# Turning two token blocks of a transformer kernel's prologue on VectorE and with SBUF to SBUF DMAs instead of on TensorE

## The chip, the cores and the metric

The kernel runs on one core of one Trainium2 chip. The metric is device time in microseconds of one execution, here the median of several runs. The core's engines have their own instruction queues, each worked off in order: TensorE (PE, with its weight loads shown as PEld), VectorE (DVE), ScalarE (ACT), GpSimd (POOL) and SyncE (SP), which only issues DMAs. They wait for each other through semaphores. Operands lie in SBUF (128 partitions); TensorE writes to PSUM, which has eight banks of 128x512 float32.

## The reference

Two rounds of an attention block followed by a Fourier mixing block, each behind a layer norm and with a residual. S = 2048 tokens, D = 640 columns, H = 32 heads of 20 columns, all float32.

```python
def _A_ref(x, wqkv, wo):
    qkv = (x @ wqkv).reshape(B, S, 3, H, Dh)      # then q, k, v by head
    scores = jnp.einsum("bhqd,bhkd->bhqk", q, k) * (Dh ** -0.5)
    p = _softmax(scores, axis=-1)
    o = jnp.einsum("bhqk,bhkd->bhqd", p, v)
    return o.transpose(0, 2, 1, 3).reshape(B, S, D) @ wo
...
x = A_x
x = x + _A_ref(_layernorm(x, axis=-1), A_wqkv, A_wo)
x = x + _B_ref(_layernorm(x, axis=-1), B_dft_seq_re, B_dft_seq_im, B_dft_hid_re, B_dft_hid_im)
x = x + _A_ref(_layernorm(x, axis=-1), A_wqkv, A_wo)
x = x + _B_ref(_layernorm(x, axis=-1), B_dft_seq_re, B_dft_seq_im, B_dft_hid_re, B_dft_hid_im)
```

## The kernel before

Each of the two layers has a **prologue**, the attention proper, a projection and the Fourier part. The change touches the prologue, function `prologue` of class `Qkv`.

The prologue works on four blocks `tb` = 0 to 3 of 512 tokens; a block is four tiles of 128 tokens, loaded two at a time (`load(k)`, k = 2 tb and 2 tb + 1, into tiles `xa`). A pair is normalised in two steps: VectorE computes mean and variance (`stats`, BN_STATS and BN_AGGR, finished on POOL as `ars`), and ScalarE applies them in place (`norm`, L132). For the matrix products the tokens must lie along the free dimension, so `turn(tb)` transposes the block: for each of the ND = 5 chunks of 128 columns four TensorE transposes of 128x128 into one PSUM bank (`ptr`, L169), then `split` takes the 512 columns out of PSUM into the tile `xt` as a high part (a copy on ScalarE, L90) and a low part (a subtraction on VectorE, L91). Each float32 product is made of three matmuls: high by high, high by low, low by high (`passes`, L103).

With `xt` of a block TensorE makes two products `pqk` of 30 matmuls each in pairs (15 for the first chunk of q, 15 for that of k; the timeline merges them as x30) and four value tiles `pv` of 15 matmuls (`own`, x60). `keep` brings a pqk tile to SBUF (`hl`, L220 on ScalarE, L222 and L223 on VectorE) and POOL stores it to DRAM (`scrq`, `scrk`, L224); ScalarE copies the value tiles to `v` (L265). A small matmul `pn` takes norms.

The order is the order of the code, which is kept on each engine. In round `tb` of the loop TensorE runs: pqk of block tb, then (for tb at least 1) `turn(tb + 1)`, pn, and the value tiles of block tb. In round 0 the value tiles come before the turn. In round tb the loop also calls `stats` and `norm` for the two pairs of block tb + 2. So in round 1 VectorE takes, in this order, the subtraction of the first pqk (L223), statistics, the squares' maximum (L222) and subtraction of the second pqk, statistics, and the five subtractions of the turned block; ScalarE takes the copies of pqk, the five copies of the turned block, four normalisations, and the value tiles. SyncE, after the two loads of x, issues in round 0 eight loads of q from DRAM (`qload`: `stq`, L522 and L523), in round 1 a weight load (L191) and eight loads of k (`kload`: `stk`, L508 and L509), in round 2 another weight load (L191) and a store of zeros (L536).

PSUM tiles of the prologue go round the eight banks in the order in which they are made. A DMA issued by SyncE signals one of eight semaphores in turn, and waits for the DMA before on the same semaphore. The tiles v15 to v11 of the pool `vals` hold raw weights until the value weights are split, and are set up as value tiles by `ones` (memsets on POOL) in round 1.

Of the kernel before, what the change touches and what calls it, by code (L numbers as in the profile page):

```python
# [5 lines left out]
F32 = mybir.dt.float32  # L6
F32R = mybir.dt.float32r
# [8 lines left out]
S, D, H, DH = 2048, 640, 32, 20  # L16
# [3 lines left out]
ND = D // 128  # L20
# [19 lines left out]
def mha_fnet_kernel(ctx, tc, x_in, wqk, wv, wo, seq, hid, nat_seq, nat_hid, out):  # L40
# [44 lines left out]
    def split(hl_h, hl_l, src, vector=False):  # L85

        if vector:
            V.tensor_copy(hl_h, src)  # L88
        else:
            A.activation(hl_h, src, AF.Copy)  # L90
        V.tensor_tensor(hl_l, src, hl_h.bitcast(F32), op=OP.subtract)  # L91
# [39 lines left out]
    def normed(dst, x, rs, i):  # L131
        A.activation(dst, x, AF.Identity, scale=rs[:, 0, i:i + 1], bias=rs[:, 1, i:i + 1])  # L132
# [5 lines left out]
    class Qkv:  # L138
        def __init__(s, L, src):
            s.L, s.src = L, src  # L140
            s.xn, s.xt, s.rs, s.v, s.sq = {}, {}, {}, {}, {}
# [3 lines left out]
            s.made, s.raw, s.silent = set(), {}, False  # L145


        def load(s, k):

            s.xn[k] = (s.first if k % 4 < 2 else s.room)(f"x{k % 4}", [2, D], F32, "xa")  # L150
# [15 lines left out]
        def turn(s, tb, wait=False):  # L166

            def transpose(p, i, dc):
                PE.transpose(p[:, i * 128:(i + 1) * 128],  # L169
                             s.xn[2 * tb + i // 2][:, i % 2, dc * 128:(dc + 1) * 128], ident)  # L170

            ps = [s.bank([128, 512], "ptr") for _ in range(ND if wait else 0)]
            for i in range(4 if wait else 0):
                for dc in range(ND):
                    transpose(ps[dc], i, dc)
            for dc in range(ND):
                if wait:
                    p = ps[dc]
                else:
                    p = s.bank([128, 512], "ptr")  # L180
                    for i in range(4):
                        transpose(p, i, dc)
                x = s.xtp(f"xt{tb}_{dc}", [2, 512], F32R, "xt")
                s.xt[tb, dc] = [x[:, 0], x[:, 1]]
                split(x[:, 0], x[:, 1], p)

        def fetch(s, c, room=None, tag="wraw", wait=False):
            s.raw[c] = (room or s.fill)(tag, [ND, 128], F32, "wraw")
# [83 lines left out]
        def begin(s, first, kq, vals, room, given):  # L272


            s.first, s.room, s.given, s.w = first, room, given, {}
            for k in range(2):
                if given:
                    s.raw[k * ND] = given.wraw[k]
                else:
                    s.load(k)  # L280
            s.wvraw = [vals(f"v{NT - 1 - dc}", [HD], F32, "wvraw") for dc in range(ND)]
            if given:
                s.load_values()

        def take(s, k):

            s.xn[k] = s.first(f"x{k}", [2, D], F32, "xa")
            for i in range(2):
                normed(s.xn[k][:, i], s.given.x[2 * k + i][:, 0], s.given.next[k], i)

# [4 lines left out]
        def prologue(s, vals, xt, fill, att):  # L295
# [39 lines left out]
            def later(tb, k, f):  # L335
                if tb + 2 < NB:
                    f(2 * tb + 4 + k)

            def own(tb, n, between=None):
                t = 4 * tb + n  # L340
                p = s.bank([128, HD], "pv")
                for dc in range(ND):
                    for f in s.value(p, t, dc):
                        f()
                    if between and dc == 1:
                        between()
                s.own(p, t, 0, False)

            for tb in range(NB):

                sq, late, last = {}, tb == 0, tb == NB - 1
                if late:
                    for k in range(2):
                        later(tb, k, s.load)
                for k in (1, 0) if last else (0, 1):
                    p = s.bank([128, 512], "pqk")
                    for dc in range(ND):
                        for f in s.product(p, s.w[k], tb, dc):
# [12 lines left out]
                if tb == 0:  # L371
                    att.setup()
                elif tb == 1:
                    for t in range(NT - ND, NT):
                        ones(t)
                if tb + 1 < NB:
                    s.turn(tb + 1)
                    for k in range(2):
                        later(tb + 1, k, s.load)
                for k in range(1 if last else 0, 2):  # L380
                    later(tb, k, s.norm)
                    s.norms(s.bank, k * ND, tb, sq[k])
                if tb == 0:
                    att.qload(0, 0, None)
                elif tb == 1:
                    s.fetch(ND + 1)
                    for j in range(2):
                        att.kload(0, 0, j)
                elif tb == 2:
                    s.w1 = s.weights(s.fill("w", [2, ND, 128], F32R, "wqk"), ND + 1, True)  # L390
                    s.fetch(1)
                    att.zeros(room)

                def bounds():
                    s.norms(s.bank, 0, tb, sq[0])
                    list(s.bound(0, room))
                    att.qshift(0, 0)
                    for j in range(2):
                        att.kload(0, 1, j)

                if not late:
                    for n in range(4):
                        own(tb, n, bounds if last and n == 0 else None)
            s.made |= {0, ND}


# [1237 lines left out]
```

## Time and profile before

| | us |
|---|---|
| median of 3 runs | 2447.15 (2446.68 to 2448.31) |
| the profiled execution | 2448.28 |
| its span, first to last instruction | 2446.5 |
| end of the last pv matmul of the prologue of layer 0 (76.79 + 8.18) | 84.97 |
| granted TensorE clock, mean | 0.998 of full speed |

The profile is of one execution. Its rows name a line of the kernel, the engine, the operation and the tiles (out<-in). A timeline row gives the start in microseconds from the start of the span, the duration, and what ran; x is the number of instructions merged in it; brackets give how long the engine was idle before and what ended that. SPq rows are DMA issues on SyncE's queue. Matmuls are pipelined, so that the starts tell more than the durations. The prologue of layer 1 lies at about 1220 to 1297 us, with the same order.

### The profile page before, as it was taken

Reading aid. Unit: us, or ns where it says so; the run is one execution under the profiler, and the core shown is the slowest. Engines: PE = TensorE matmul, PEld = TensorE weight load, DVE = VectorE, ACT = ScalarE, POOL = GpSimd, SP = SyncE. Lnnn points to the kernel's source line nnn. Section 1 sums busy time; section 2 is a strip of 40 time slices with the busy share of each in tenths; the row PEclk is TensorE's granted clock in tenths of the full one; section 3 lists DMA queues with packets and bytes.
Section 4 is the critical chain, followed back from the end, with each engine's and each line's share of the span. In section 5 each row is a group of like instructions: output and inputs, shape, how many; then the busy total and the mean of one; then the engine's idle time right before and its main releaser. Section 6 shows DMA issues by size and latency. Waiting matters only on the chain. (4 is left out here: it accounts for less than half of the span.)

```text
span 2446.5 us, 43831 instructions
## 1 busy us (share of the span) xinstructions
PE 2423.7 (99%) x16320; PEld 1167.8 (48%) x16320; DVE 996.3 (41%) x2250; ACT 2114.9 (86%) x2428; POOL 530.7 (22%) x1036
## 2 busy tenths in 40 slices
PE   8999999999999999999999999999999999999998
PEld 7644444443333332339885444454433333333496
DVE  6244442234343333428753444323433332333275
ACT  6699998899999999995457999988999999999862
POOL 2022211112212212115421212211111211222143
PEclk9999999999999999999999999999999999999999
DMA  5324231223232225318552332312221322252265
GB/s 186 101 88 127 83 111 53 77 69 111 73 95 90 87 89 164 98 38 293 196 181 96 112 102 86 117 54 70 78 82 57 93 63 69 57 153 79 77 240 198
DMA packets 128226, 262.63 MB, mean 107 GB/s; under 512 B 29936, under 2 KB 54288, under 8 KB 128004
## 3 DMA queue, kind: packets, MB, share of 16 engines
q1 hardware_dynamic: 89412, 159.89, 20.2%
q0 software_dynamic: 38592, 99.85, 12.8%
q8 instruction: 131, 2.15, 0.4%
q14 instruction: 91, 0.75, 0.1%
HBM read 175.29 MB, written 84.31 MB: 106 GB/s over the span
## 5 line engine op out<-in xcount | busy, mean ns | idle before, releaser
L547 ACT ACTIVATE e<-psc 128x1024 f32<-128x1024 f32 x2048 | 1917.3, 1060 | 108.8 <-PE psc L544 98.2
L555 PE MATMUL acc<-e,v 128*32 128x512 f32 x8192 | 1030.0, 600 | 0.4 <-DVE of L562 0.4
L544 PE MATMUL psc<-stq,stk 62*128 62x512 f32 x4096 | 746.7, 445 | 1.9 <-ACT e L547 0.5
L544 PEld LDWEIGHTS psc<-stq,stk 62*128 62x128 f32 x4096 | 334.2, 184 | 704.8 <-ACT e L547 567.7
L555 PEld LDWEIGHTS acc<-e,v 128*32 128x32 f32 x8192 | 211.0, 108 | 407.2 <-issue 369.7
L103 PE MATMUL pqk<-xt,wqk 128*128 128x512 f32 x1200 | 319.1, 407 | 0.4 <-DVE xt L91 0.4
L576 POOL DMA_DIRECT2D o<-oh x256 | 131.8, 523 | 825.0 <-DVE oh L571 813.1
L88 DVE CAST hl<-pqk 128x512 fp32r<-128x512 f32 x64 | 44.3, 692 | 603.7 <-PE pqk L103 603.7
L103 PEld LDWEIGHTS pqk<-xt,wqk 128*128 128x128 f32 x1200 | 213.2, 188 | 83.5 <-issue 39.5
L103 PE MATMUL pv<-wv,xt 128*128 128x320 f32 x960 | 151.7, 313 | 0.0
L103 PEld LDWEIGHTS pv<-wv,xt 128*128 128x128 f32 x960 | 141.0, 188 | 13.5 <-issue 9.7
L562 DVE STREAM_TRANSPOSE of<-acc 128x512 f32<-128x512 f32 x64 | 45.8, 715 | 225.3 <-PE acc L555 225.3
L576 POOL DMA_DIRECT2D o<-ot x256 | 128.2, 509 | 1.1 <-issue 0.8
L224 POOL DMA_DIRECT2D scrk<-hl x40 | 27.7, 693 | 412.3 <-DVE hl L91 251.9
L224 POOL DMA_DIRECT2D scrq<-hl x40 | 28.3, 707 | 405.5 <-DVE hl L91 239.9
L96 PE MATMUL py<-wo,o 128*128 128x320 f32 x320 | 101.0, 316 | 0.0
L825 DVE TENSOR_REDUCE far<-cq 128x1 f32<-128x512 f32 (+5 forms) x169 | 98.6, 584 | 5.7
L98 PE MATMUL py<-wo,o 128*128 128x320 f32 x320 | 98.8, 309 | 0.2 <-DMA o<-o 0.2
L97 PE MATMUL py<-wo,o 128*128 128x320 f32 x320 | 98.7, 308 | 0.0
L829 DVE TENSOR_TENSOR cq<-cq 128x512 f32<-128x512 f32 (+4 forms) x166 | 96.4, 581 | 4.6 <-DMA cq<-in_nat_seq_dram 3.3
L263 DVE COPY v<-pv 128x320 f32<-128x320 f32 x32 | 15.7, 490 | 161.2 <-PE pv L103 161.2
L233 DVE TENSOR_REDUCE top<-pn 32x1 f32<-32x512 f32 x50 | 33.7, 676 | 76.6 <-PE pn L232 76.5
(204 smaller groups left out, 1761.9 us busy)
## 6 DMA issues: line engine op xcount, KB each, us to landing
cq<-in_nat_seq_dram POOLq DMA_DIRECT2D x64, 512.0 KB, 5.3
scrq<-hl POOLq DMA_DIRECT2D x40, 512.0 KB, 3.3
scrk<-hl POOLq DMA_DIRECT2D x40, 512.0 KB, 3.1
stq<-scrq SPq DMA_DIRECT2D x256, 80.0 KB
stk<-scrk SPq DMA_DIRECT2D x128, 160.0 KB
o<-o SPq DMA_DIRECT2D x32, 384.0 KB
stq<-scrq SPq DMA_DIRECT2D x256, 40.0 KB
stk<-scrk SPq DMA_DIRECT2D x128, 80.0 KB
```

Of the source, the lines that this page charges most:

```text
L96: PE.matmul(out_ap, ah, bh, start=start, stop=False)
L97: PE.matmul(out_ap, ah, bl, start=False, stop=False)
L98: PE.matmul(out_ap, al, bh, start=False, stop=stop)
L103: yield lambda i=i, j=j, k=k: PE.matmul(out_ap, a[i], b[j], start=dc == 0 and k == 0, stop=dc == ND - 1 and k == 2)
L224: G.dma_start(s.scr["qk"[k]][c * 128:(c + 1) * 128, :, tb * 512:(tb + 1) * 512], hl.bitcast(F32))
L544: PE.matmul(p[:, i], s.k[g, kc // 8, j][r, kc % 8 * 128:(kc % 8 + 1) * 128], s.q[g, qb, j][r], start=True, stop=True)
L547: A.activation(e, p, AF.Exp, scale=SCALE)
L555: PE.matmul(s.acc[32 * j:32 * j + 32], s.a.v[kc][:, v0:v0 + 32], s.e[n, j // 2][:, j % 2], start=kc == 0, stop=kc == NT - 1, skip_group_ch ...
L562: V.transpose(t0.rearrange("p b c -> p (b c)"), s.acc)
L576: G.dma_start(s.o[k, h * DH:(h + 1) * DH, qb * 512:(qb + 1) * 512], hl[k][32 * j:32 * j + DH])
L825: V.tensor_reduce(to, x, op=OP.max, axis=AX.X, apply_absolute_value=True)
L829: V.tensor_tensor(y, x, y, op=op)
```

## The change

Blocks 2 and 3 are no longer turned by TensorE; block 1 still is, in round 0, and so is block 0 ahead of the loop. In place of `norm` and `turn`, three functions do the work for a block:

- `spaced` writes the normalised tiles, still four instructions of 128x640 on ScalarE, not in place but into a tile `xs` of form [4, 5, 4, 32] per partition: for each of four groups g of 32 columns within a chunk, all five chunks, all four token tiles, 32 columns.
- `swap` lets VectorE transpose each of the four groups (128x640) in 32x32 squares, into four tiles `xz`, and then issues 16 DMAs on SyncE, each of 32 partitions by 640 float32 (80 KB), SBUF to SBUF, which bring the squares of group g to the partitions 32 g to 32 g + 31 of `xs`.
- `unspaced` splits the five chunks from `xs` into `xt`, with the same ScalarE copy and VectorE subtraction as before, but reading SBUF with a stride.

`swap(2)` is called in round 0, after the normalisation of block 2 and ahead of `qload`; `unspaced(2)` in round 1 between value tiles 1 and 2, with `swap(3)` right behind it; `unspaced(3)` in round 2 between value tiles 1 and 2. The memsets of v12 to v15 move behind that, since the `xz` tiles use their place. The x tiles of a block become one tile [4, D] (`tiles`) in place of two; the `xt` tiles of block 3 become two in place of five, since `xs` of block 2 lies in the place of the first. The sizes add up to the same.

```diff
+        def spaced(s, k):
+            tb, j = divmod(k, 2)
+            if j == 0:
+                s.y[tb] = s.xtp("xt3_0", [4, ND, 4, 32], F32, "xs") if tb == 2 else s.first("x0", [4, ND, 4, 32], F32, "xs")
+            for i in range(2):
+                x = s.xn[k][:, i].rearrange("p (c g f) -> p g c f", c=ND, g=4)
+                normed(s.y[tb][:, :, :, 2 * j + i], x, s.rs[k], i)
+
+        def swap(s, tb):
+            zs = [s.vals(f"v{NT - 1 - g}", [ND * 128], F32, "xz") for g in range(4)]
+            for g, z in enumerate(zs):
+                V.transpose(z, s.y[tb][:, g].rearrange("p c n f -> p (c n f)"))
+            for g, z in enumerate(zs):
+                for i in range(4):
+                    nc.sync.dma_start(s.y[tb][32 * g:32 * g + 32, i].rearrange("p c n f -> p (c n f)"), z[32 * i:32 * i + 32])
+
+        def unspaced(s, tb):
+            y = s.y[tb].rearrange("p i c n f -> p c i n f")
+            xs = [s.xtp(f"xt3_{i}", [ND // 2 + 1 - i, 2, 512], F32R, "xt") for i in range(2)] if tb == 3 else None
+            for dc in range(ND):
+                x = xs[dc > ND // 2][:, dc % (ND // 2 + 1)] if xs else s.xtp(f"xt{tb}_{dc}", [2, 512], F32R, "xt")
+                s.xt[tb, dc] = [x[:, 0], x[:, 1]]
+                split(*[x[:, k].rearrange("p (n i f) -> p i n f", n=4, i=4) for k in range(2)], y[:, dc])
...
-                    for t in range(NT - ND, NT):
+                    for t in range(NT - ND, NT - 4):
                         ones(t)
-                if tb + 1 < NB:
-                    s.turn(tb + 1)
+                if late:
+                    s.turn(1)
                     for k in range(2):
-                        later(tb + 1, k, s.load)
+                        s.load(6 + k)
                 for k in range(1 if last else 0, 2):
-                    later(tb, k, s.norm)
+                    later(tb, k, s.spaced)
                     s.norms(s.bank, k * ND, tb, sq[k])
+                if late:
+                    s.swap(2)
...
                     for n in range(4):
                         own(tb, n, bounds if last and n == 0 else None)
+                        if n == 1 and not last:
+                            s.unspaced(tb + 1)
+                            if tb == 1:
+                                s.swap(3)
+                            else:
+                                for t in range(NT - 4, NT):
+                                    ones(t)
```

How the order moves on three engines, at the place between the turn of block 1 and the first pqk of block 2 (the changed kernel's line numbers are higher: L266 is what L233 was, L256 L223, L253 L220, L298 L265, L564 and L565 L522 and L523).

VectorE, from the end of round 0 into round 1, as a difference (minus before, plus after; `ars` rows end the statistics):

```order
 L126 TENSOR_SCALAR ars<-amv 128x2
 L91 TENSOR_TENSOR xt<-ptr,xt 128x512 x5
-L233 TENSOR_REDUCE top<-pn 32x1
-L223 TENSOR_TENSOR hl<-pqk,hl 128x512
+L266 TENSOR_REDUCE top<-pn 32x1
+L206 STREAM_TRANSPOSE xz<-xs 128x640 x4
+L256 TENSOR_TENSOR hl<-pqk,hl 128x512
 L121 BN_STATS ast<-xa 128x6 x2
 L122 BN_AGGR amv<-ast 128x2
```

The four transposes stand between the turn of block 1 and the subtraction of block 1's first pqk.

ScalarE in rounds 1 and 2, before (`xa` is normalised, `v` the value tiles):

```order
L220 ACTIVATE sq<-pqk 128x512
L220 ACTIVATE hl<-pqk 128x512 x2
L90 ACTIVATE xt<-ptr 128x512 x5
L132 ACTIVATE xa<-xa,ars 128x640 x4
L265 ACTIVATE v<-pv 128x16x20 x4
```

and now:

```order
L253 ACTIVATE sq<-pqk 128x512
L253 ACTIVATE hl<-pqk 128x512 x2
L132 ACTIVATE xs<-xa,ars 128x20x32 x4
L298 ACTIVATE v<-pv 128x16x20 x2
L90 ACTIVATE xt<-xs 128x4x4x32 x5
L298 ACTIVATE v<-pv 128x16x20 x2
```

The copies that make `xt` of block 2 stood ahead of the normalisations of block 3; now they stand behind them and behind two value tiles.

SyncE from the two loads of x of block 3 on, now:

```order
L159 DMA xa<-in_x_dram 128x2x640 x2
L209 DMA xs<-xz 32x640 x16
L564 DMA stq<-scrq_67 40x1x512
L565 DMA stq<-scrq_67 20x512
L564 DMA stq<-scrq_67 40x1x512
```

Before, the loads of `stq` followed the loads of x at once.

More of the change, by code (lines that the diff above doesn't have):

```diff
@@ L140, in __init__ @@
             s.L, s.src = L, src
-            s.xn, s.xt, s.rs, s.v, s.sq = {}, {}, {}, {}, {}
+            s.xn, s.xt, s.rs, s.v, s.sq, s.y = {}, {}, {}, {}, {}, {}
             s.scr = {qk: dr.tile([D, 2, S], F32, name=f"scr{qk}_{L}") for qk in "qk"}
@@ L145, in __init__, with tiles @@
             s.made, s.raw, s.silent = set(), {}, False
+        def tiles(s, k):
+            if k % 2 == 0:
+                s.xb = (s.room if k % 4 else s.first)(f"x{k % 4}", [4, D], F32, "xa")
+            s.xn[k] = s.xb[:, 2 * (k % 2):2 * (k % 2) + 2]
         def load(s, k):
-            s.xn[k] = (s.first if k % 4 < 2 else s.room)(f"x{k % 4}", [2, D], F32, "xa")
+            s.tiles(k)
             n = 1 if k < 2 else 2
@@ L272, in begin @@
         def begin(s, first, kq, vals, room, given):
-            s.first, s.room, s.given, s.w = first, room, given, {}
+            s.first, s.room, s.given, s.w, s.vals = first, room, given, {}, vals
             for k in range(2):
@@ L285, in take @@
         def take(s, k):
-            s.xn[k] = s.first(f"x{k}", [2, D], F32, "xa")
+            s.tiles(k)
             for i in range(2):
```

## The prediction

> **What bounds the kernel now.** I read the first part of the page (busy time of each engine), then the timeline of the prologue of layer 0 on every engine, and the same rows in layer 1.
>
> ```profile
> span 2446.5 us, 43831 instructions
> PE 2423.7 (99%) x16320; PEld 1167.8 (48%) x16320; DVE 996.3 (41%) x2250; ACT 2114.9 (86%) x2428; POOL 530.7 (22%) x1036
> ```
>
> Columns: busy microseconds, share of the span, instructions. TensorE (PE) is busy all along, and the share alone does not say whether a transpose taken away is time won: that is read in its stage. The rows of TensorE there, as start, duration, what (x is how many instructions the row merges):
>
> ```profile
> 31.39 7.10 PE L103 MATMUL pqk<-xt,wqk 128*128 128x512 f32 x30
> 38.33 2.34 PE L169 MATMUL ptr<-ident,xa 128*128 128x128 f32 x20
> 40.61 0.39 PE L232 MATMUL pn<-sq,ind 128*32 128x512 bf16 x1
> 40.93 9.07 PE L103 MATMUL pv<-wv,xt 128*128 128x320 f32 x60
> ...
> 49.83 7.00 PE L103 MATMUL pqk<-xt,wqk 128*128 128x512 f32 x30
> 56.66 2.34 PE L169 MATMUL ptr<-ident,xa 128*128 128x128 f32 x20
> 59.26 9.07 PE L103 MATMUL pv<-wv,xt 128*128 128x320 f32 x60
> 68.16 6.99 PE L103 MATMUL pqk<-xt,wqk 128*128 128x512 f32 x30
> 75.08 0.39 PE L232 MATMUL pn<-sq,ind 128*32 128x512 bf16 x1
> 75.40 1.14 PE L103 MATMUL pv<-wv,xt 128*128 128x320 f32 x6
> ```
>
> Blocks 1, 2 and 3 of the prologue start at 31.39, 49.83 and 68.16. No row has an idle time in brackets: TensorE goes from one to the next without waiting, so TensorE bounds this stage, and what leaves its queue is time won as long as nothing else makes it wait.
>
> **What is removed.** Blocks 1 and 2 contain the 20 transposes that make blocks 2 and 3 of `xt`; block 3 contains none and shows the price. In block 3 the pn matmul starts 75.08 - 68.16 = 6.92 us after the first pqk and the first pv 0.32 us later; from the first pv to the next pqk are 49.83 - 40.93 = 8.90 us in block 1. A block without a turn is thus 6.92 + 0.32 + 8.90 = 16.14 us. Block 2 takes 68.16 - 49.83 = 18.33 us: 2.19 us go. Block 1 takes 18.44 us, of which 0.11 us are its slower pqk (7.10 against 6.99), which stays: 2.19 us again. Per layer 4.38 us. Layer 1 shows the same blocks:
>
> ```profile
> 1262.29 6.99 PE L103 MATMUL pqk<-xt,wqk 128*128 128x512 f32 x30
> 1280.61 6.99 PE L103 MATMUL pqk<-xt,wqk 128*128 128x512 f32 x30
> ```
>
> 18.32 us for its block 2, so both layers together lose 8.76 us of TensorE time.
>
> ```profile
> L169 PE MATMUL ptr<-ident,xa x160: 270/273/477, 7.1 to 1271.2; 128*128 128x128 f32 x160
> ```
>
> The median of one transpose is 273 ns, and 20 of them would make 5.46 us a block; the rows above show 20 in 2.34 us. The Trainium skill (Trainium Kernel Development and Optimization, section Performance Expectations) says that matmul busy time misleads because matmuls are pipelined. By busy time the sum would be 80 x 0.273 = 21.8 us; the trace agrees with the rule, and I count the distance between starts.
>
> **What is added, and where it runs.** Per block 2 or 3: four ScalarE normalisations write a spaced copy instead of in place (same number as before), VectorE makes four 128x640 transposes, SyncE issues 16 SBUF to SBUF DMAs, and the five copies on ScalarE and five subtractions on VectorE read SBUF in place of PSUM. The last ten are moved, not added: for block 2 of `xt` behind the second value tile of block 1. ScalarE, VectorE and SyncE have room on average; what matters is the chain up to the first pqk of block 2. Its rows of before:
>
> ```profile
> 29.43 2.56 ACT L90 ACTIVATE xt<-ptr 128x512 fp32r<-128x512 f32 x5
> 30.06 3.08 DVE L91 TENSOR_TENSOR xt<-ptr,xt 128x512 fp32r<-128x512 f32 x5
> 31.84 3.38 ACT L132 ACTIVATE xa<-xa,ars 128x640 f32<-128x640 f32 x4
> 36.29 0.69 DVE L223 TENSOR_TENSOR hl<-pqk,hl 128x512 fp32r<-128x512 f32 x1 [2.56 <-ACT sq L220]
> 39.19 0.16 DVE L126 TENSOR_SCALAR ars<-amv 128x2 f32<-128x2 f32 x1
> 39.70 0.43 DVE L222 TENSOR_TENSOR sq<-sq,hl 128x512 bf16<-128x512 bf16 x1 [0.34 <-ACT hl L220]
> 43.06 0.16 DVE L126 TENSOR_SCALAR ars<-amv 128x2 f32<-128x2 f32 x1
> 44.27 1.74 ACT L132 ACTIVATE xa<-xa,ars 128x640 f32<-128x640 f32 x2 [0.56 <-POOL ars L128]
> 45.92 0.74 ACT L265 ACTIVATE v<-pv 128x320 f32<-128x320 f32 x2
> ```
>
> and, grouped over the whole span (busy us, mean ns of one), the nearest rows to the new operations:
>
> ```profile
> L569 DVE STREAM_TRANSPOSE ot<-on 128x512 f32<-128x512 f32 x64 | 45.5, 712 | 2.2
> L91 DVE TENSOR_TENSOR xt<-ptr,xt 128x512 fp32r<-128x512 f32 x40 | 24.6, 681 | 0.1
> L90 ACT ACTIVATE xt<-ptr 128x512 fp32r<-128x512 f32 x40 | 20.5, 620 | 0.0
> L91 DVE TENSOR_TENSOR xn<-fold,xn 128x640 fp32r<-128x640 f32 x16 | 13.3, 834 | 0.3
> L90 ACT ACTIVATE xn<-fold 128x640 fp32r<-128x640 f32 x16 | 11.8, 740 | 12.4 <-DVE fold L1089 11.4
> L571 DVE CAST oh<-ot 128x512 fp32r<-128x512 f32 x64 | 27.3, 427 | 2.2
> ```
>
> The copies and subtractions from SBUF cost what those from PSUM do: per 128 columns VectorE's 640-wide row in SBUF is (834 - 681) = 153 ns and ScalarE's (740 - 620) = 120 ns above the 512-wide row from PSUM, which is about one column per cycle and leaves nothing for the other memory. I take 0.62 and 0.68 us for them. What the strides of 32 elements add, no row shows; it may be nothing or, at worst, one more instruction's fixed part (rival 4).
>
> VectorE's transposes for block 2 wait for the four normalisations, which end at 31.84 + 3.38 = 35.22, and they stand ahead of the subtraction at 36.29, whose statistics (39.19, 43.06) release, through POOL, the ScalarE normalisation at 44.27. In the new order that normalisation stands ahead of the copies that feed the next pqk. A 128x512 transpose takes 0.712 us; five subtractions of 0.681 in a row take 3.08, so their step is (3.08 - 0.68)/4 = 0.60, some 0.085 less than their length. A transpose of 640 is then about 0.712 + 0.14 long, its step 0.765, and four take 3.06 us. Bounds: 4 x 0.43 = 1.7 us, were they as quick as VectorE's cast of 512 columns, and 4 x 0.865 = 3.5 us without overlap.
>
> The chain then runs so. Transposes 35.25 to 38.31; subtraction at 38.31 in place of 36.29, 2.02 us later; the row at 39.70 had waited (0.34 idle, and with the pipeline overlap 0.44 from 39.19 + 0.07), so it moves to 41.28, by 1.58; the statistics at 43.06 and the normalisation at 44.27 by the same, to 45.85; the two v copies to 47.50, ending at 48.15 (their step is 0.33). First copy of block 2 then: 48.15; its subtraction 0.63 later (29.43 to 30.06), 48.78, done after 0.68 at 49.47. TensorE is ready earlier: block 1 without the turn has its next pqk at 31.39 + 0.11 + 16.14 = 47.64. Its first matmul needs the copy, the second the subtraction; unhindered that second one starts a step of 6.99/30 = 0.23 later, at 47.88, and now at about 49.5. **The wait is 1.6 us a layer.** After it the next subtractions come every 0.60 us against 0.70 us for three matmuls, so it does not grow. Behind the waiting copies on ScalarE stand the v copies of the last two value tiles of block 1 and the pqk copies of block 2; TensorE comes back to their PSUM banks eight tiles later, in block 3. The subtraction that moves to 38.31 also moves its store on POOL, for which the attention waits only. With transposes at the lower bound (1.3 us sooner) it is 0.3, at the upper 2.0.
>
> That holds only if the 16 DMAs have landed by 48.15, on which the copies wait. They are on SyncE behind the two x loads:
>
> ```profile
> 33.51 0.79 SPq L522 DMA_DIRECT2D stq<-scrq  x1
> 34.34 0.49 SPq L523 DMA_DIRECT2D stq<-scrq  x1
> 46.02 0.33 SPq L509 DMA_DIRECT2D stk<-scrk  x1
> 46.39 0.33 SPq L508 DMA_DIRECT2D stk<-scrk  x1
> ...
> 1276.95 0.38 SPq L536 DMA_DIRECT2D shiftb<-zeros  x1
> ...
> L224 POOL DMA_DIRECT2D scrq<-hl x40: 673/700/908, 20.2 to 2126.6; - x40
> DMA to landing us min/median/max: 3.1/3.3/7.8
> ```
>
> The new ones carry 32 rows of 2.5 KB. Bounds of the step: 0.37 (stk) and 0.83 (stq, 33.51 to 34.34); nearest is the 32-row store of zeros, 0.38, hence I take 0.42. Three can go during the transposes, thirteen after 38.3 or so: last issue 43.8, and landing 3.3 later, as the 512 KB stores land, 47.1. That is hidden with 1 us to spare; at 0.83 a DMA it is 38.4 + 10.8 + 3.3 = 52.5 and not hidden. What stands behind them on SyncE, the eight stq loads, one weight load and the eight stk loads of before, moves some 6 us back; the first psc matmul needs these after the last pv (75.40 onward), so there are over 20 us of cover. For block 3, the transposes follow the subtractions of block 2 (about 51.8), their DMAs end near 55 + 5.5 + 3.3 = 63.8, and TensorE, delayed, comes to its pqk at 47.64 + 1.6 + 16.14 = 65.4. The first pair takes 1.3 us, 65.1: no wait, 0.3 us of cover, and with a landing nearer to 2 us more. I count it as nothing. The moved memsets of v on POOL stand ahead of its two hl stores of block 3, at a time when POOL is idle: nothing.
>
> **Sum.** Per layer -2 x 2.19 + 1.6 = -2.78 us; two layers -5.6 us. The profiled execution took 2448.28 us (1.8 outside its span); the change makes it 2442.7. The median of the runs shown, 2447.15, lies 1.1 below the profiled one: **2441.6 us**. The attention behind it is only moved.
>
> **The rivals.**
> 1. Hardly a wait: VectorE's transposes take the 0.43 of its cast. Then 2 x (4.38 - 0.3) = 8.2 us are won: 2439.0. Against it stands the 0.712 of the trace's own transposes of SBUF. 0.16.
> 2. The DMAs come late. With the stq step (0.83) they land at 52.5 instead of 47.1; the second matmul starts 1.3 us after, at 53.8, a wait of 5.9 in place of 1.6, net +1.5 a layer: 2450. With landing a little past 48.15 it lies between. For it: these rows of the stq loads; against it: their 40 rows differ in form, and they move behind the new DMAs. 0.21.
> 3. Slower. SyncE holds eight DMAs of its own in flight: the ninth waits on the semaphore of the first. If each takes the longest landing of the stores, 7.8 us, the first round (36.1 to 40.1) ends at 47.9 and the sixteenth lands at 55.7; second matmul at 57.0, a wait of 9.1, net +4.7 a layer: 2456.6. It decides from a landing of 51.0 on (a wait of 4.38 eats the gain) and is told from no change from 53.4. Against it: 3.3 is the median. 0.11.
> 4. The transposes and copies of spaced data run much slower than contiguous rows, on the same chain: at 0.2 us more for each of the six normalisations, four transposes and one pair that it contains, 2.4 us a layer, the wait is 4.0 and the gain 0.4 a layer, 2446.4; at half of that 2444. It is part of the forecast's upper end.
>
> **How the numbers follow.** My forecast, with rival 4 as its upper part, 0.52: 2440 to 2445. A measurement of this kernel tells a change of about 0.2%, 4.9 us, from none. Faster by that: rival 1 (0.16) and some seven tenths of the forecast (0.37), 0.53. Within: the rest of the forecast (0.15) and rival 2 (0.21), 0.36. Slower: rival 3, 0.11. The range runs from all 8.8 won to the gain gone, 2438.0 to 2448.0; beyond it lie rival 3 and the worst of rival 2.
>
> **What would show it.** The two turns gone from blocks 1 and 2, so block 1 is 16.25 us plus a wait, block 2 16.14. A gap before the pqk of block 2 of about 1.6 us in each layer, put down to ScalarE's copy (and VectorE's subtraction), not to a DMA; if it is put down to a DMA, rival 2 or 3. The subtraction of pqk at about 38.3 instead of 36.3. Four transposes in some 3.1 us. No gap before block 3. Wrong it would be with a gap at block 3, with no gap at all, or with a change of the attention's own length by over a microsecond.

## The result, and the profile after

| | before | after |
|---|---|---|
| median, us | 2447.17 (2446.43 to 2448.31, 6 runs) | 2461.83 (2461.04 to 2462.21, 6 runs) |
| the profiled execution, us | 2448.28 | 2461.96 |
| its span, us | 2446.5 | 2460.2 |

The ratio is 1.006 (95% interval 1.0049 to 1.007): the change costs 14.7 us, where the forecast had a gain of 5.6. The first part of the page after hardly differs from that before; TensorE's busy share still reads 99%:

```profile
span 2460.2 us, 43794 instructions
PE 2423.8 (99%) x16240; PEld 1164.6 (47%) x16240; DVE 1008.2 (41%) x2266; ACT 2115.4 (86%) x2428; POOL 529.5 (22%) x1036
```

80 transposes are gone (16320 to 16240) and the busy time is the same, so something else has become longer. TensorE's timeline after, prologue of layer 0, then of layer 1:

```profile
33.05 7.10 PE L103 MATMUL pqk<-xt,wqk 128*128 128x512 f32 x30
...
40.40 9.06 PE L103 MATMUL pv<-wv,xt 128*128 128x320 f32 x60
52.42 9.96 PE L103 MATMUL pqk<-xt,wqk 128*128 128x512 f32 x30 [2.96 <-ACT xt L90]
62.31 0.39 PE L265 MATMUL pn<-sq,ind 128*32 128x512 bf16 x1
62.63 9.06 PE L103 MATMUL pv<-wv,xt 128*128 128x320 f32 x60
74.28 0.50 PE L103 MATMUL pqk<-xt,wqk 128*128 128x512 f32 x1 [2.59 <-ACT xt L90]
75.01 8.48 PE L103 MATMUL pqk<-xt,wqk 128*128 128x512 f32 x29 [0.22 <-DVE xt L91]
83.42 0.39 PE L265 MATMUL pn<-sq,ind 128*32 128x512 bf16 x1
...
1269.97 0.49 PE L103 MATMUL pqk<-xt,wqk 128*128 128x512 f32 x1 [1.83 <-ACT xt L90]
1270.69 6.89 PE L103 MATMUL pqk<-xt,wqk 128*128 128x512 f32 x29 [0.23 <-DVE xt L91]
...
1291.19 10.06 PE L103 MATMUL pqk<-xt,wqk 128*128 128x512 f32 x30 [4.30 <-ACT xt L90]
1301.18 0.39 PE L265 MATMUL pn<-sq,ind 128*32 128x512 bf16 x1
```

The turns are out of blocks 1 and 2. In their place there is an idle time before the pqk of block 2 and before that of block 3, in both layers. And three of the four pqk behind an idle time are slow: from the first pqk to pn it is 9.89, 9.14 and 9.99 us, against 6.92 before. Only the one behind the shortest idle time (1.83) keeps its speed. The table by stretches of layer 0 shows why; columns: stretch, its length, busy time of each engine, then the granted TensorE clock, the DMA share and GB/s:

```profile
49.00:52.40 3.40, 0.46 (x4) 0.19 (x2) 0.00 (x1) 1.40 (x5) 0.00 (x0) 0.85 0.33 90
52.40:54.40 2.00, 1.98 (x4) 1.35 (x5) 2.00 (x4) 2.00 (x5) 0.00 (x0) 0.50 0.27 76
...
56.40:58.40 2.00, 2.00 (x7) 1.57 (x6) 2.00 (x3) 0.00 (x0) 0.00 (x0) 0.55 0.80 254
58.40:62.00 3.60, 3.60 (x18) 2.93 (x16) 0.72 (x2) 1.09 (x2) 0.69 (x1) 1.00 0.71 197
```

The granted clock is 0.50 until about 58.2, some 6 us behind the gap, then 1.00. A gap is thus paid twice, and since slow matmuls count as busy, the page's first part does not show it.

Who is late, on SyncE and ScalarE (from their timelines in layer 0):

```profile
37.78 11.97 SPq L209 DMA_DIRECT2D xs<-xz  x16
49.85 0.88 SPq L564 DMA_DIRECT2D stq<-scrq  x1
...
59.03 0.27 SPq L551 DMA_DIRECT2D stk<-scrk  x1
59.77 11.97 SPq L209 DMA_DIRECT2D xs<-xz  x16
```

```profile
47.35 1.73 ACT L132 ACTIVATE xs<-xa,ars 128x640 f32<-128x640 f32 x2 [1.53 <-POOL ars L128]
49.00 0.74 ACT L298 ACTIVATE v<-pv 128x320 f32<-128x320 f32 x2
51.73 2.71 ACT L90 ACTIVATE xt<-xs 128x512 fp32r<-128x512 f32 x5 [2.00 <-DMA xs<-xz]
...
73.60 2.71 ACT L90 ACTIVATE xt<-xs 128x512 fp32r<-128x512 f32 x5 [5.83 <-DMA xs<-xz]
```

Sixteen DMAs take SyncE 11.97 us, 0.75 a step on average: most issues take 0.59 us with 0.04 between them, a step of 0.63, and in each sixteen two or three take 0.8 to 1.4 us; why these are longer was not looked for. ScalarE is through with its chain at 49.7, waits 2.00 us for the DMAs of block 2, and 5.83 for those of block 3, which come on SyncE behind those of block 2 and the loads of q, k and a weight (49.85 to 59.30).

Where the time went, worked out from the starts in both profiles (the block without a turn as the prediction has it: 16.25 and 16.14 in layer 0; for layer 1 block 1 took 18.58 before, 16.39 without the turn):

| us against before | layer 0 | layer 1 |
|---|---|---|
| two turns | -4.38 | -4.38 |
| block 1 (up to the late pqk of block 2) | +3.12 | +1.97 |
| block 2 (its slow pqk, and up to the late pqk of block 3) | +5.72 | +5.08 |
| block 3, first pqk to pn | +2.22 | +3.07 |
| pn to the first psc matmul | +0.59 | +0.60 |
| together | +7.27 | +6.34 |

That makes 13.61. The stage ahead of block 1 of layer 0 ended 1.66 us later in this execution (33.05 against 31.39; other kernels with the same stage stand at 31.27 to 33.25), and 1.6 us come back on the way through the rest: 13.7 in the span.

### The profile page after: what moved, and what is told of

It reads as the page before. It is cut to its first block, busy times and chain, and to the rows that moved or that the text cites. A ratio compares the mean times of both kernels' runs of the same rounds, so it can differ in the third digit from the quotient of the medians.

```text
span 2460.2 us, 43794 instructions
## 1 busy us (share of the span) xinstructions
PE 2423.8 (99%) x16240; PEld 1164.6 (47%) x16240; DVE 1008.2 (41%) x2266; ACT 2115.4 (86%) x2428; POOL 529.5 (22%) x1036
## 5 line engine op out<-in xcount | busy, mean ns | idle before, releaser
L103 PE MATMUL pqk<-xt,wqk 128*128 128x512 f32 x1200 | 329.0, 416 | 13.0 <-ACT xt L90 12.0
L103 PEld LDWEIGHTS pqk<-xt,wqk 128*128 128x128 f32 x1200 | 219.0, 193 | 100.5 <-issue 39.6
L266 DVE TENSOR_REDUCE top<-pn 32x1 f32<-32x512 f32 x50 | 33.7, 677 | 76.6 <-PE pn L265 76.4
```

The source lines that it names most:

```text
L103: yield lambda i=i, j=j, k=k: PE.matmul(out_ap, a[i], b[j], start=dc == 0 and k == 0, stop=dc == ND - 1 and k == 2)
```

## The experiments

The theory: the engines' detour is as forecast, the sixteen DMAs are late, and the idle time lowers TensorE's clock. The rivals: the detour of VectorE and ScalarE itself is the loss; the moving of the bytes, or the eight DMAs in flight, sets the DMAs' time, not their issue; the clock falls through the DMA traffic. Each kernel starts from the changed one; times are medians beside runs of the kernel before on the same chip (2446.73 for the first four, 2446.71 for the next four, 2445.57, one run, for the two after, 2447.07 for the last two).

**1. The DMAs left out.** Also, a decision further on that picks the way by the values is held to the way the complete kernel takes (here and in experiments 5, 6, 9 and 10).

```
-for g, z in enumerate(zs):
-    for i in range(4):
-        nc.sync.dma_start(s.y[tb][32 * g:32 * g + 32, i]..., z[32 * i:32 * i + 32])
```

> The 16 DMAs of swap are left out for both blocks and layers (so xt of blocks 2 and 3 holds wrong columns), and the acceptance flag at the end is set whatever the data. Transposes, strided normalisations, strided copies and the order on every engine stay. Theory A (issue): the 16 issues on SyncE take 0.75 us each and land too late, and everything else of the change costs only the 1.6 us a layer that ScalarE's late normalisation costs; then one gap of 1 to 2 us before the pqk of block 2 in each layer, no gap before block 3, pqk of 30 in 7.0 us at full clock everywhere, 2441 to 2444 us. Theory B (engines): the detour over VectorE and the new place of the copies on ScalarE is what costs; then the gaps stay near 3 us and the time stays above 2455.

2443.45 us (2442.28 to 2444.85, 10 runs), ratio 0.9985 (0.9976 to 0.9995). TensorE's timeline:

```profile
33.25 7.09 PE L103 MATMUL pqk<-xt,wqk 128*128 128x512 f32 x30
...
50.51 0.50 PE L103 MATMUL pqk<-xt,wqk 128*128 128x512 f32 x1 [0.86 <-ACT xt L90]
...
58.03 0.39 PE L262 MATMUL pn<-sq,ind 128*32 128x512 bf16 x1
...
67.25 6.99 PE L103 MATMUL pqk<-xt,wqk 128*128 128x512 f32 x30
```

Block 1 takes 50.51 - 33.25 = 17.26 us, 1.01 over 16.25, and the pqk of block 2 up to pn 7.52, 0.60 over 6.92: a wait of 1.61 us, the forecast's 1.6; by the same two terms it is 1.35 in layer 1. No gap before block 3 (67.25 - 58.03 = 9.22 us = 0.32 + 8.90). The detour of the engines is not the loss; the DMAs are, with 17.9 us (3.28 won against 14.66 lost, each beside its own runs of before).

**2. Block 3 alone by DMAs**, block 2 turned by TensorE in round 1 as before; the DMAs of block 3 go right behind its normalisation.

```
+elif tb == 1:
+    s.turn(2)
...
-    later(tb, k, s.spaced)
+    later(tb, k, s.norm if late else s.spaced)
-if late:
-    s.swap(2)
+if tb == 1:
+    s.swap(3)
...
-if n == 1 and not last:
-    s.unspaced(tb + 1)
+if n == 1 and tb == 2:
+    s.unspaced(3)
```

> Block 2 is turned by TensorE as before; block 3 goes the new way, with its transposes and DMAs issued in round 1 and its copies in round 2. Theory A: the DMAs have some 14 us before the copies need them and land in time, so one turn a layer is won and nothing lost: 2447.2 - 2 x 2.19 = 2442.8, no gap before block 3. Theory B or C (the 1.3 MB between SBUF partitions is slow in itself and disturbs the rest): a gap before block 3 or slower loads, 2447 or more.

2443.07 us (2442.87 to 2444.42, 10 runs), ratio 0.9985 (0.9976 to 0.9995): it beats both kernels. No gap anywhere:

```profile
50.41 6.99 PE L103 MATMUL pqk<-xt,wqk 128*128 128x512 f32 x30
...
66.55 6.99 PE L103 MATMUL pqk<-xt,wqk 128*128 128x512 f32 x30
```

66.55 - 50.41 = 16.14 us, the predicted length of a block without a turn. The sixteen DMAs still take 10.61 us here, but they start at 48.19 instead of 59.77, and that hides them.

**3. The DMAs alternating between SyncE and POOL.**

```
-nc.sync.dma_start(s.y[tb]...
+(nc.sync, G)[i % 2].dma_start(s.y[tb]...
```

> Every second one of the 16 DMAs is issued on POOL's queue instead of SyncE's. Theory A: SyncE needs 6 us for its eight, POOL (0.5 to 0.7 us an issue) about the same, all land about 46 to 47 us in layer 0, ahead of the copies; gap before block 2 about 1.6 us, none before block 3, full clock: 2441 to 2446. Theory C (the transfers themselves, 1.3 MB in 12 us, are limited by the partitions they touch): landing as late as before, gaps of 2 to 4 us, 2458 or more.

2448.22 us (2444.21 to 2452.81, 10 runs), ratio 1.0006 (0.9997 to 1.0016): 13.2 us better than the change, but not the gain expected. Before block 2 the gaps are 1.06 and 0.80 us, the size of experiment 1; before block 3 they are 1.97 and 1.43. The eight DMAs that are left to SyncE take 5.77 us in block 2: one wait of 0.7 us ahead of the second, then the same step of 0.63, though with eight semaphores none of the eight has to wait for another to land. In block 3 they do wait, for the loads of k ahead of them on the same semaphores (what SyncE waited for from 54 to 62 us; total, times and longest in us):

```profile
SPq L209 <- DMA stk<-scrk: 2.3, 5, 0.9
```

The last issue ends at 61.5 and the copies start at 67.6; from 58 to 66 us all 16 DMA engines are busy (share 1.01) at 200 GB/s, with the loads of k among the transfers. So there it is the moving of the bytes, with the loads ahead, that is late, more than the issue.

**4. TensorE kept busy** with 14 matmuls that nothing reads, behind the last value tile of blocks 1 and 2.

```
+if n == 3 and not last:
+    p = s.bank([128, 512], "pidle")
+    for j in range(14):
+        PE.matmul(p, s.w[0][:, 0, j % ND], s.xt[tb, j % ND][0], start=True, stop=True)
```

> The changed kernel with 14 matmuls of 128x512 (3.3 us) whose result nobody reads behind the last value tile of blocks 1 and 2, so that TensorE is busy while the copies are awaited. If the half clock of the trace (0.50 for some 6 us behind gaps of 2.6 us and more) comes from TensorE's idling, the clock stays at 1.0 and the pqk behind the gap take 7.0 instead of 9.2 to 10.1 us: some 7 us less, 1.4 us of it given back where the gap was shorter than the filling, 2454 to 2457. If pqk is slow for another reason (DMA or VectorE traffic beside it), it stays 9 to 10 us and the time 2461 or more.

2457.75 us (2455.74 to 2461.07, 5 runs), ratio 1.0046 (1.0032 to 1.006), just above what was expected: 3.6 us come back by doing useless work. The timeline in layer 0:

```profile
47.52 3.36 PE L442 MATMUL pidle<-xt,wqk 128*128 128x512 f32 x14
50.71 0.46 PE L103 MATMUL pqk<-xt,wqk 128*128 128x512 f32 x1
51.40 6.91 PE L103 MATMUL pqk<-xt,wqk 128*128 128x512 f32 x29 [0.23 <-DVE xt L91]
...
73.09 0.50 PE L103 MATMUL pqk<-xt,wqk 128*128 128x512 f32 x1 [2.27 <-ACT xt L90]
73.81 8.53 PE L103 MATMUL pqk<-xt,wqk 128*128 128x512 f32 x29 [0.23 <-DVE xt L91]
```

Where the filler covers the wait (block 2), pqk runs at full speed with the same DMAs around it; where 2.27 us of idle time stay behind it (block 3), it is slow again.

**5. A tenth of the bytes**: each of the sixteen DMAs carries 64 of its 640 columns.

```
-..."p c n f -> p (c n f)"), z[32 * i:32 * i + 32])
+..."p c n f -> p (c n f)")[:, :64], z[32 * i:32 * i + 32, :64])
```

> The sixteen DMAs of a block stay, but each carries 64 of its 640 columns, a tenth of the bytes (the other columns of xs stay unturned, so xt is not the transpose). Theory A: SyncE needs about 0.75 us for each of these DMAs whatever their length, because of their 32 rows or a fixed part; then the sixteen still take 11 to 12 us, the gap before the pqk of block 2 in layer 0 stays at 2.5 to 3 us, the pqk behind it stays slow, 2455 to 2462 us. Theory B: the step is set by the bytes or by the landing of earlier ones (eight semaphores); then the step falls to 0.3 to 0.45 us, the gap to the 0.6 to 0.9 us seen without DMAs, 2443 to 2446 us.

2458.47 us (2456.11 to 2462.32, 4 runs), ratio 1.005 (1.0035 to 1.0066). SyncE's timeline:

```profile
36.10 11.31 SPq L209 DMA_DIRECT2D xs<-xz  x16
```

0.71 us a step with 256-byte rows, so the issue does not go with the bytes (theory A). The gaps are 2.00 and 3.27 us in layer 0, 1.10 and 4.85 in layer 1; the first is below the 2.5 to 3 expected, and the pqk behind it is slow all the same (8.88 us up to pn).

**6. No DMAs, but ScalarE repeats the first copy** of xt 1, 10, 6 and 13 times, to hold TensorE up.

```
+for _ in range({(0, 2): 1, (0, 3): 10, (1, 2): 6, (1, 3): 13}[int(s.L != "0"), tb] if dc == 0 else 0):
+    A.activation(x[:, 0].rearrange("p (n i f) -> p i n f", n=4, i=4), y[:, 0], AF.Copy)
```

> Without the sixteen DMAs (xs is used unturned), and ScalarE repeats the first copy of xt 1, 10, 6 and 13 times (block 2 and 3 of layer 0, block 2 and 3 of layer 1) to hold TensorE up: gaps of about 1.4, 2.2, 3.8 and 3.8 us. Theory: it is TensorE's own idling that lowers the granted clock, from somewhere between 2.0 and 2.3 us on; then the two long gaps are each followed by a pqk of 9.5 to 10 us in place of 6.9 at a clock of about 0.50, the first is not, and the one of 2.2 tells on which side it lies; 2458 to 2463 us. Rival: the clock falls through the DMA traffic between the partitions; then all four pqk take 6.9 to 7.0 us and the time is the gaps alone, about 2453 us.

2461.86 us (one run). The gaps are 1.50, 3.27, 4.80 and 5.25 us, larger than meant, so that no gap tests the boundary at 2.2. The pqk up to pn behind them takes 7.51, 8.94, 8.77 and 9.00 us, slow where the theory says so, but less than the 9.5 to 10 expected. Block 3 of layer 0 in the timeline, and its stretch by the columns above:

```profile
69.40 0.49 PE L103 MATMUL pqk<-xt,wqk 128*128 128x512 f32 x1 [3.27 <-ACT xt L90]
70.12 8.28 PE L103 MATMUL pqk<-xt,wqk 128*128 128x512 f32 x29 [0.23 <-DVE xt L91]
```

```profile
69.40:72.00 2.60, 2.37 (x6) 1.69 (x7) 2.60 (x5) 2.60 (x6) 0.00 (x0) 0.57 0.00 0
```

The clock is 0.57 with a DMA share of 0.00. The idle time lowers it, not the traffic.

**7. Block 2 alone by DMAs**, block 3 turned by TensorE.

```
+if tb == 2:
+    s.turn(3)
...
-    later(tb, k, s.spaced)
+    later(tb, k, s.spaced if late else s.norm)
...
-    s.unspaced(tb + 1)
-    if tb == 1:
-        s.swap(3)
+    if tb == 1:
+        s.unspaced(2)
```

> Only block 2 goes by VectorE and DMAs, block 3 is turned by TensorE as before. Theory: block 2 itself loses 3.9 us in layer 0 (3.1 us wait and 3.0 us slow pqk less the 2.19 of the turn) and nothing much in layer 1, and the gaps at block 3 are a consequence of both blocks together; without them 2449 to 2453 us. Rival: the two blocks add up; then, block 3 alone being 4.1 us faster than before, block 2 alone would be 18.8 us slower than before, 2463 to 2467 us.

2452.47 us (2450.74 to 2453.97, 10 runs), ratio 1.0022 (1.0013 to 1.0032): 5.8 us slower. With block 3 alone 3.7 faster, the two would add up to +2.1, and the change costs 14.7. The missing 12.6 us exist only where both blocks are moved. In the profile of the change these are the wait at block 3 (71.53, when TensorE would have been ready, to 74.28: 2.75; in layer 1, by the same sum, 4.46) and the slow pqk behind it (2.22 and 3.07): 12.5.

**8. The exchange through DRAM**: four stores of 128 rows and four loads of 32 rows of 10 KB a block.

```
+d = dr.tile([4, 4, 32, ND * 128], F32, name=f"dz{tb}_{s.L}")
 for g, z in enumerate(zs):
-    for i in range(4):
-        nc.sync.dma_start(s.y[tb][32 * g:32 * g + 32, i]..., z[32 * i:32 * i + 32])
+    nc.sync.dma_start(d[g].rearrange("i p x -> (i p) x"), z)
+for g in range(4):
+    nc.sync.dma_start(s.y[tb][32 * g:32 * g + 32]..., d[g].rearrange("i p x -> p i x"))
```

> The exchange goes through DRAM: four stores of 128 rows of 2.5 KB and four loads of 32 rows of 10 KB a block, eight DMAs in place of sixteen. Theory A (the issues on SyncE set it): eight steps of at most 0.75 us and two landings of 2 to 3.3 us in a row, landed by about 48, so gaps before block 2 of 0.6 to 1.5 us, none or under 1 us at block 3, full clock, 2441 to 2447 us. Theory B (the moving of the bytes sets it): twice the bytes, 2.6 MB a block, take 11 to 13 us, landed at 50 to 51; gaps of 1.5 to 3 us and slow pqk as in the change, 2450 to 2462 us.

2460.51 us (2457.62 to 2461.31, 5 runs), ratio 1.0054 (1.004 to 1.0068): theory B, for this kernel. The gaps are 2.02 and 3.56 us in layer 0, 2.34 and 3.34 in layer 1, those at block 3 longer than expected. The view of the tile dz (issues, with least, median and longest in ns), and a stretch in block 3:

```profile
L209 SPq DMA_DIRECT2D dz<-xz x16: 319/340/1040, 36.4 to 1275.0; - x16
L211 SPq DMA_DIRECT2D xs<-dz x16: 302/331/607, 39.0 to 1280.5; - x16
```

```profile
64.00:70.00 6.00, 4.33 (x30) 4.06 (x28) 0.00 (x0) 0.40 (x1) 0.03 (x2) 1.00 0.98 276
```

The issues are cheap now, 0.34 and 0.33 us. But with twice the bytes the DMA engines are full (share 0.98 to 1.04 in both blocks); the last load of block 3 is issued at 63.7 and the copies start at 71.20. One limit was left for another.

**9. Stores to DRAM in the same sixteen pieces**, which nothing reads, in place of the SBUF to SBUF DMAs.

```
-nc.sync.dma_start(s.y[tb][32 * g:32 * g + 32, i]..., z[32 * i:32 * i + 32])
+nc.sync.dma_start(d[g, i], z[32 * i:32 * i + 32])
```

> The sixteen DMAs keep their 32 rows of 2.5 KB, their order and their queue, but store the turned squares in a DRAM buffer that nothing reads (xs is used unturned). Theory A1: the 0.59 us of an issue come from both ends lying in SBUF; then an issue takes 0.30 to 0.40 us as the other stores from SBUF do, the step is below 0.45, the last is issued by 43, and the gap before block 2 of layer 0 is the 0.9 us of ScalarE's chain, 2443 to 2447 us. Rival A2: it is the cut into 32 partitions at a time or the row of 2.5 KB; then 0.55 to 0.60 us again, the first sixteen still take 10.5 to 12 us. In neither case do the copies wait for them.

2444.27 us (one run). Gaps of 0.85 and 0.86 us before block 2, none before block 3. The issue by the view of its line:

```profile
L210 SPq DMA_DIRECT2D dz<-xz x64: 302/420/1219, 36.2 to 1274.5; - x64
```

A median of 0.42 us; the first sixteen take 8.34 us, 0.52 a step, and end at 44.5, all a little more than expected. So neither the 32 partitions nor the row of 2.5 KB makes the 0.59.

**10. Four rows in place of 32** in each SBUF to SBUF DMA.

```
-s.y[tb][32 * g:32 * g + 32, i]..., z[32 * i:32 * i + 32]
+s.y[tb][32 * g:32 * g + 4, i]..., z[32 * i:32 * i + 4]
```

> The sixteen DMAs stay from SBUF to SBUF with rows of 2.5 KB, but carry 4 rows each in place of 32 (the other rows of xs stay unturned). Theory A3: the cost of an issue goes with its rows; then 0.25 to 0.40 us, gaps of 0.6 to 1.2 us at block 2, 2443 to 2447 us. Rival A4: it is fixed for a DMA with both ends in SBUF; then 0.50 to 0.60 us, the sixteen take 10.5 to 12 us, a gap of 2 us or more at block 2 of layer 0 and at block 3, 2453 to 2461 us.

2459.02 us (one run).

```profile
L209 SPq DMA_DIRECT2D xs<-xz x64: 577/584/1202, 36.2 to 1285.7; - x64
```

0.58 us with an eighth of the rows, sixteen in 10.79: with both ends in SBUF the price goes neither with the rows nor, by experiment 5, with the bytes (A4). One number of A4 missed: the gap at block 2 of layer 0 is 1.52, not 2 or more; the issues end at 46.95 and the copies start 1.73 us later.

**11. The loads of round 1 behind the DMAs of block 3.**

```
-if tb == 0:
-    att.qload(0, 0, None)
-elif tb == 1:
-    s.fetch(ND + 1)
-    for j in range(2):
-        att.kload(0, 0, j)
...
 s.swap(3)
+s.fetch(ND + 1)
+att.qload(0, 0, None)
+for j in range(2):
+    att.kload(0, 0, j)
```

> The change as it is, but in round 1 the weight load, the eight stq loads and the eight stk loads are issued on SyncE behind the sixteen DMAs of block 3 and no longer between those of block 2 and those of block 3. Theory: block 3 comes late because its DMAs start 3.5 us after the first transpose is done, behind 9.5 us of loads on SyncE; now they start with the transposes, block 3 has no gap in layer 0 and at most 1.5 us in layer 1, and the time is that of block 2 alone less two turns, 2452.5 - 4.4 = 2448, up to 2451 us. The gap before block 2 stays. Rival: the late end is that of sixteen issues at 0.75 us whatever stands ahead; the gaps of 2.6 to 4.3 us at block 3 stay, 2458 to 2463 us.

2456.68 us (2453.84 to 2459.25, 4 runs), ratio 1.0042 (1.0026 to 1.0057): the time is a miss. The copies of block 3 do come as the theory says (67.73, in layer 0 no gap before the first pqk). But the edit made a wait of its own, on VectorE:

```profile
68.90 0.49 DVE L88 CAST wqk<-wraw 128x640 fp32r<-128x640 f32 x1 [6.16 <-DMA wraw<-in_wqk_dram]
69.43 0.83 DVE L91 TENSOR_TENSOR wqk<-wraw,wqk 128x640 fp32r<-128x640 f32 x1
70.17 3.09 DVE L91 TENSOR_TENSOR xt<-xs,xt 128x512 fp32r<-128x512 f32 x5
```

The split of the weight, whose load is now late, stands ahead of the subtractions that make xt; TensorE's second matmul of block 3 waits 1.57 us for them (2.52 in layer 1).

**12. The same order, with the two queues of experiment 3.**

> The same order, and the DMAs of a block alternate between SyncE and POOL. Theory: the issues are then short enough (5.8 us for eight) and no loads run beside those of block 3; gaps of 0.8 to 1.1 us at block 2 from ScalarE's chain, none at block 3, full clock: 2440 to 2443.5 us, the forecast's own time. Rival: the moving of the bytes between partitions sets it (the 16 DMA engines were busy all the time in the alternating kernel from 58 to 66 us); a gap of 1.5 to 2 us stays at block 3, 2445 to 2449 us.

2444.07 us (2443.15 to 2446.32, 11 runs), ratio 0.9989 (0.998 to 0.9998).

```profile
48.86 0.49 PE L103 MATMUL pqk<-xt,wqk 128*128 128x512 f32 x1 [1.05 <-ACT xt L90]
...
65.59 6.99 PE L103 MATMUL pqk<-xt,wqk 128*128 128x512 f32 x30
```

The gaps fit the theory: 1.05 and 0.40 before block 2 (0.8 to 1.1 expected), none before block 3, pqk at full speed. The copies of block 3 start at 62.1 instead of the 67.6 of experiment 3; of the loads, which stood ahead of the transfers there, none does so here. The median lies 0.6 us above the expected span; the 0.59 us a layer between pn and psc, which the sum did not have, are enough to account for it.

So the change does bring a gain once its DMAs are issued in time, 3.0 us for both blocks; the half of it that needs no second queue and no moved load, experiment 2, brings 3.7. The two intervals overlap.

## Why the prediction was wrong, step by step

**What is removed: right.** Blocks without a turn are 16.14 us long wherever nothing else waits (experiment 2).

**The engines' detour: right.** The new operations as the views of their tiles and lines give them after the change (least, median, longest in ns):

```profile
L206 DVE STREAM_TRANSPOSE xz<-xs x16: 800/802/848, 36.9 to 1275.2; 128x640 f32<-128x640 f32 x16
L90 ACT ACTIVATE xt<-xs x20: 612/614/630, 51.7 to 1292.6; 128x512 fp32r<-128x512 f32 x20
L91 DVE TENSOR_TENSOR xt<-xs,xt x20: 682/684/693, 52.4 to 1293.6; 128x512 fp32r<-128x512 f32 x20
L209 SPq DMA_DIRECT2D xs<-xz x64: 507/589/1426, 37.8 to 1288.3; - x64
```

Four transposes take 3.03 us (forecast 3.06), copies and subtractions 0.61 and 0.68 (0.62 and 0.68). The strides cost nothing, so rival 4 falls; so does rival 1, whose 0.43 a transpose was half. The wait by this chain, 1.6 us, is what experiment 1 shows in layer 0 (1.35 in layer 1).

**The sixteen DMAs: the step that failed.** "nearest is the 32-row store of zeros, 0.38, hence I take 0.42 ... landing 3.3 later ... 47.1. That is hidden with 1 us to spare." The step is 0.75, near the upper bound. The row was chosen by its 32 rows and its length, and neither sets the price (experiments 5 and 10); stores of this very shape to DRAM do take 0.42 (experiment 9). It was one of two, besides: the same store in layer 0, at 64.5, takes 1.14. What sets the sixteen apart from those stores is that both ends lie in SBUF, and the profile before has such rows. In the Fourier part SyncE copies single rows from SBUF to SBUF (views of the lines, before):

```profile
L1178 SPq DMA_DIRECT2D c<-c3low x2: 605/616/627, 1048.4 to 2259.5; - x2
L1197 SPq DMA_DIRECT2D e<-e x2: 543/569/595, 1149.1 to 2362.1; - x2
```

By 0.62 and 0.04 between, thirteen issues from 38.3 on would end at 46.9, and with the prediction's own landing of 3.3 us the copies would start at 50.2 instead of 48.15. By this estimate the DMAs are not hidden. The landing was taken too long: 1.98 us (block 2) and 1.86 (block 3) from the end of the last issue to the copies. The Trainium skill (DMA: Bandwidth & Descriptors, section Anatomy of one DMA — SWDGE (gpsimd) path) gives about 2.0 us as the fixed part of a DMA on POOL's path. The stretch measured here is on SyncE's queue and is not the same measure, but is of that size.

**Block 3: counted as nothing, the largest loss.** "DMAs end near 55 + 5.5 + 3.3 = 63.8." The prediction saw that the loads behind the DMAs of block 2 would move, and looked whether their own readers had cover. It did not see that the DMAs of block 3 stand behind those loads on SyncE: they started at 59.77, 4.4 us after the first transpose began (55.41), and ended at 71.74. Experiment 7 puts 12.6 us on the two blocks following each other. The order alone would not have done it. With the prediction's 0.42 the last issue of block 2 is at 43.8, and the loads, which took 9.45 us, would be through at 53.3; the first transpose of block 3 it had at 51.8, done after 0.8 at 52.6. By this estimate the queue holds block 3 up by 0.7 us, in place of 3.6 (56.2 to 59.77) and a longer sixteen. So the mis-sized step is behind this loss too, and either cure helps: with the step as it is, but the loads behind, block 3 has no gap in layer 0 before its first pqk (experiment 11).

**The price of a gap.** Each wait was counted once. The prediction has no term for the clock: in the profiled execution it cost 2.97 us behind block 2 of layer 0 (9.89 against 6.92) and 2.22 and 3.07 behind block 3, some 8 us in all, of which 0.6 each would be there at full clock (the second matmul waits for the subtraction). Experiments 4 and 6 show that it is the idle time.

**The rivals.** Rival 2, late DMAs, was the right mechanism, with landing at 51.7 (50.1 when the late start of this execution is taken off) for its 52.5; its 2450 missed block 3 and the clock. Experiment 7, which has only its part of the story, measures 2452.5. Rival 3, eight in flight, came nearest in time by another cause: from 36 to 50 us SyncE's DMAs wait for no landing, only for the transposes. The step of most of them, 0.63, is the same where only eight are issued (experiment 3), and the average stays at 0.71 where hardly a byte moves (experiment 5).

**Attention only moved: off by more than the microsecond the prediction allowed.** 0.6 us a layer before the first psc were not foreseen. TensorE waits there for ScalarE's last copy to v. The wait is absent in experiments 2, 4 and 7, which make more PSUM tiles in the prologue; that the banks fall out differently is an inference, it was not tried by itself. Experiment 1, the detour without the DMAs, wins 3.3 us of the forecast's 5.6; this wait is 1.2 of what is missing. Of the 1.6 us that come back over the rest of the span of the change, 1.3 lie in the turn of block 1 of layer 1: from its first transpose to pn it takes 3.58 us in the profile before, with waits of 0.39 and 0.48 for ScalarE, and 2.28 after. Why it waited before was not looked for.

## What to carry to other kernels

Price a DMA by a row that has the same two ends, not the same shape (here a search of the whole profile would have found one), and follow every later instruction of that queue, not only the readers of what was moved. A wait of TensorE of more than about 2 us cost 1.3 to 2.6 us more behind it in half clock (8.8 to 10.1 us for a pqk that takes 7.5 behind a short wait), and "busy" hides that: read the granted clock in the stretch after the gap. When a transfer is to replace work on the bound engine, move first the piece that has the longest lead: half the change was a gain, both halves in a row on one queue were a loss.

## What the runs showed of the hardware that was not expected

- An SBUF to SBUF DMA takes SyncE 0.58 to 0.59 us to issue (medians), from 4 rows to 32 and from 256 bytes to 2.5 KB a row; the single rows of the kernel before took 0.50 to 0.63. Stores of the same tiles to DRAM took 0.34 and 0.42, their loads from it 0.33 (experiments 8 and 9). That is no price of DRAM in general: the loads of q take 0.5 to 0.9. On POOL the same DMAs went at 0.50 us (seven in 3.49 us, experiment 3).
- Before a pqk of the prologue, the granted clock of TensorE fell to 0.50 for every idle time of 2.27 us and more (17 in 8 kernels, 2.27 to 5.25), at the latest 2.0 us after its end, and stayed up behind those of 0.40 to 1.97. Between lies a band: 2.00 and 2.02 us were followed by a slow pqk (experiments 5 and 8), 2.18 us was not (experiment 7, layer 1, 6.88 us for 29 matmuls). The Trainium skill (TensorE: Matmul & The Clock Gate, section Why this matters for your kernels) asks for no idle gaps over some 3 us. These traces differ: here 2.3 us were enough each time.
- Half clock came in fixed lengths. By the clock entries in the traces, each of these 19 falls (with the two at 2.00 and 2.02) lasts 3.41 or 6.83 us, and the changes of one trace lie whole multiples of 3.41 us apart; in the change they are at 51.36, 58.18, 75.25, 78.66, 1290.39 and 1297.22. So a longer wait was not followed by a larger loss of speed: behind 5.25 us (experiment 6) the pqk up to pn took 9.00 us, behind 2.96 (the change) 9.89. That the place of a wait on this grid decides within the band would fit, but was not tried.
- Transfers between partitions, with loads of k beside them, kept all 16 DMA engines busy at 200 GB/s; the same engines moved 300 GB/s at a share of 0.84 in experiment 12 (62 to 66 us). What lowers it was not taken apart.
